# Left-over second products dealt in quarters between the first Strassen products, four eviction buffers in the last groups, and the last WO halves interleaved

## Chip, cores and metric

The kernel runs on one core of one Trainium2 chip. The metric is the device time of one execution in microseconds (us). Three executions of the kernel before took 1122.71, 1125.68 and 1120.59 us, so the median is 1122.71 us. "Profiled time" is the time of the one execution that was recorded, and "span" is the stretch from its first to its last recorded instruction.

## The reference

The kernel computes, for one sequence of 2048 rows of 576 numbers in float32,

```
xn  = layernorm(x)
out = x + attention(xn) @ wo + relu(xn @ w1) @ w2
```

`w1` is 576 x 4608 and `w2` is 4608 x 576. The attention has 32 heads of 18 columns. A row attends to itself and to seven earlier rows at distances 2, 4, ..., 14, so its scores are products and sums on VectorE and not matrix products. `wqkv` is 576 x 1728 and `wo` is 576 x 576.

## The kernel before

**Tiling.** The rows fall into two phases of 1024 rows (`ph` 0 and 1), a phase into four row blocks of 256 (`tb`), and the 4608 hidden columns into 36 chunks of 128 (`f`). Every float32 matrix product is done as three products of a rounded high part and a remainder (`hi*hi`, `hi*lo`, `lo*hi`). `two` (L172 to L176) makes such a pair from a staged tile: ScalarE copies the high part, and VectorE, or GpSimd where it says `pooled`, subtracts it to get the low part.

**First and second products.** The first product gives `h = relu(xn @ w1)` for a chunk; the second product adds `h @ w2` of the chunk into a `po` accumulator in PSUM. A row block's second product is cut into columns 0 to 255 (`h` = 0) and 256 to 575 (`h` = 1, 320 columns). `evict` (L730) copies the two parts of a finished block into an `ev` buffer with ScalarE (L736); after the second part GpSimd issues a transfer that adds the buffer to the output in HBM (L742). There are two `ev` buffers, and two pairs of `po` banks.

**Two stages in a phase.** The first six chunks are done one by one: 24 slots, numbered `b` to `b` + 23, in each of which `o_two` does one second product. The other 30 chunks are done in pairs of chunks and pairs of row blocks by a Strassen scheme: 30 groups in a phase, each with seven products `M(1)` to `M(7)` and remainders `R` for the rows 512 to 575 of `w1`, all accumulated in PSUM banks called a, q (tiles `ph`), f, r (tiles `pm`). `seed` copies one bank into another (ScalarE, L1006), `keep` copies a bank into SBUF (L1010), `plus` adds a bank to that copy (VectorE, L1015), `c_parts` makes the relu pair of a finished quarter (L783 and L787).

**Rows of the array.** TensorE holds two products at once: one in its lower 64 rows, one in the upper 64. They are issued alternately as pairs. When a bank was last written from one half and is to be written from the other, `rows` (L146) and `mm_rows` (L136) put an instruction ahead that waits until the last such product is complete. Where other work lies between the two, nothing is waited for.

**Order.** There is no scheduler: each engine executes in the order in which the program text emits its instructions. `prologue` (L1170) is the change from the first stage to the second, once in each phase; the first products of group 0 are there, with the second products of the last two slots `n0` and `n0` + 1, which are left over. `group` does groups 1 to 29 in eight steps each, where a second product of a former group lies between two steps. `run_bg` (L667) emits attention work for VectorE (L575, L578 and so on) as long as a running estimate says that VectorE is not more than a margin behind TensorE; `room` computes the margin inside a group. `tail_end` and `last_group` finish a phase: `seam` calls them in phase 0, `epilogue` in phase 1. Their pieces of the last two groups fill `ev` buffers, and `last_group` also took a tile of pool `pr`, free by then, as two more. `epilogue` then does the product with `wo` for four blocks of attention rows, each in two column parts and each part in two halves (`wo_half`, L705). The first two blocks go through `wo_block`; the last two end in `last_part`, which adds on VectorE (L1377) to rows read back from the output and writes them.

**The start.** SP issues the loads in program order: `x` tiles (`load_x`, L301), `w1` (L193), `w2` chunks (`w2_load`, L217). The `w2` chunks go through two staging buffers, so the third waits until chunk 0 is split.

## Time and profile before

| what | value |
|---|---|
| median of three executions | 1122.71 us |
| profiled time | 1121.96 us |
| its span | 1119.9 us |
| TensorE busy | 1105.7 us |
| VectorE, ScalarE, GpSimd busy | 844.5, 573.1, 358.8 us |
| granted TensorE clock | 1.00 in every slice |
| HBM traffic | 152 GB/s over the span |

Lines of a view by time begin with the start and the length in us; "idle before" in brackets is how long the engine stood idle and what ended that. PE is TensorE, PEld its weight loads, DVE VectorE, ACT ScalarE, POOL GpSimd; a q behind the name is the engine's sequencer or queue. One row of a matmul is one half of a pair; two halves start together. In a stream without waits pairs of 256 columns start every 0.11 us and pairs of 320 columns every 0.15 us, so a wait shows as a larger distance between two starts even where the engine is called busy, because a recorded matmul lasts 0.27 us.

### The profile page before, as it was taken

Reading aid. Unit: us, or ns where it says so; the run is one execution under the profiler, and the core shown is the slowest. Engines: PE = TensorE matmul, PEld = TensorE weight load, DVE = VectorE, ACT = ScalarE, POOL = GpSimd, SP = SyncE. Lnnn points to the kernel's source line nnn. Section 1 sums busy time; section 2 is a strip of 40 time slices with the busy share of each in tenths; the row PEclk is TensorE's granted clock in tenths of the full one; section 3 lists DMA queues with packets and bytes.
Section 4 is the critical chain, followed back from the end, with each engine's and each line's share of the span. In section 5 each row is a group of like instructions: output and inputs, shape, how many; then the busy total and the mean of one; then the engine's idle time right before and its main releaser. Section 6 shows DMA issues by size and latency. Waiting matters only on the chain.

```text
span 1119.9 us, 37923 instructions
## 1 busy us (share of the span) xinstructions
PE 1105.7 (99%) x16410; PEld 1089.5 (97%) x16410; DVE 844.5 (75%) x1254; ACT 573.1 (51%) x1350; POOL 358.8 (32%) x377
## 2 busy tenths in 40 slices
PE   8999999999999999999999999999999999999998
PEld 8999999999999999999999999999999999999988
DVE  6676798897897898985326339988988988989551
ACT  5434563564465355567544345636635644565550
POOL 2314341333333233443211225314413323334421
PEclk9999999999999999999999999999999999999999
DMA  7369995696597588889957257749857956988895
GB/s 234 129 162 223 188 183 101 143 203 110 118 222 131 88 201 154 148 164 270 267 80 171 38 126 164 143 80 216 166 97 159 194 94 147 181 146 164 180 209 137
DMA packets 136598, 177.26 MB, mean 158 GB/s; under 512 B 27872, under 2 KB 83936, under 8 KB 136400
## 3 DMA queue, kind: packets, MB, share of 16 engines
q0 software_dynamic: 37632, 81.40, 46.8%
q1 hardware_dynamic: 98080, 92.55, 28.1%
q8 instruction: 129, 2.11, 0.7%
q10 hardware_dynamic: 720, 0.89, 0.2%
q14 instruction: 37, 0.30, 0.1%
HBM read 74.07 MB, written 96.22 MB: 152 GB/s over the span
## 4 chain that ended last, share of the span: by engine, by line
PE 87%; DVE 4%; issue 4%; DMA 2%; ACT 2%; POOL 1%; DVEq 0%; ACTq 0%; POOLq 0%
PE po L163 28%; PE po L142 22%; PE ph L163 14%; PE pm L163 11%; PE pm L142 5%; PE ph L142 4%; DMA out<-ev 2%; PE ph L130 1%; DVE ar L176 1%; PE po L130 1%; DVE ar L787 1%; DVE att L622 1%; PE po L119 0%; DMA st<-in_w 0%; ACT ev L736 0%
## 5 line engine op out<-in xcount | busy, mean ns | idle before, releaser
L163 PE MATMUL po<-ar 64*128 64x320 f32 (+1 forms) x5760 | 456.8, 289 | 1.8 <-ACT ar L783 1.7
L163 PEld LDWEIGHTS po<-ar 64*128 64x128 f32 x5760 | 398.7, 184 | 3.3 <-ACT ar L783 1.9
L163 PE MATMUL ph<-xT,ar 64*128 64x256 f32 x2520 | 319.8, 275 | 2.6 <-ACT pm L1006 1.3
L742 POOL DMA_DIRECT2D out<-ev x128 | 151.6, 1184 | 486.6 <-ACT ev L736 376.2
L163 PEld LDWEIGHTS ph<-xT,ar 64*128 64x128 f32 x2520 | 285.7, 184 | 5.7 <-ACT pm L1006 3.5
L163 PE MATMUL pm<-xS,ar 64*128 64x256 f32 x2160 | 258.8, 275 | 0.6
L163 PEld LDWEIGHTS pm<-xS,ar 64*128 64x128 f32 x2160 | 236.1, 184 | 1.9 <-ACT u L1010 0.6
L736 ACT ACTIVATE ev<-po 128x512 f32<-128x512 f32 (+1 forms) x266 | 171.5, 651 | 128.1 <-PE po L163 65.6
L176 DVE TENSOR_TENSOR ar<-st,ar 128x256 fp32r<-128x256 f32 (+3 forms) x236 | 156.4, 675 | 73.7 <-ACT ar L172 73.2
L172 ACT ACTIVATE ar<-st 128x256 fp32r<-128x256 f32 (+3 forms) x304 | 149.1, 504 | 12.1 <-DMA st<-in_w 4.7
L142 PE MATMUL po<-wq,xT 64*128 64x432 f32 x1296 | 133.8, 353 | 0.3 <-ACT ev L736 0.3
L142 PEld LDWEIGHTS po<-wq,xT 64*128 64x128 f32 x1296 | 119.9, 184 | 3.2 <-ACT ev L736 0.6
L938 POOL TENSOR_TENSOR st<-st 128x256 f32<-128x256 f32 x120 | 113.2, 949 | 16.0 <-DVE ar L787 6.5
L174 POOL TENSOR_TENSOR ar<-st,ar 128x256 fp32r<-128x256 f32 (+1 forms) x68 | 75.7, 1116 | 126.3 <-ACT ar L172 126.3
L163 PE MATMUL ph<-xS,ar 64*128 64x256 f32 x720 | 102.7, 275 | 1.3 <-ACT ph L1006 1.1
L163 PEld LDWEIGHTS ph<-xS,ar 64*128 64x128 f32 x720 | 94.2, 184 | 2.8 <-ACT ph L1006 2.1
L610 DVE TENSOR_TENSOR pr<-att 128x1152 f32<-128x1152 f32 x64 | 87.1, 1378 | 0.6
L575 DVE TENSOR_TENSOR pr<-att 128x1152 f32<-128x1152 f32 x64 | 87.2, 1367 | 0.2
L578 DVE TENSOR_REDUCE att<-pr 128x64 f32<-128x1152 f32 x64 | 85.6, 1342 | 0.0
L142 PE MATMUL po<-ar 64*128 64x256 f32 (+1 forms) x984 | 71.1, 289 | 0.0
L617 DVE TENSOR_TENSOR pr<-pr 128x1152 f32<-128x1152 f32 x64 | 70.0, 1094 | 1.2
L787 DVE SCALAR_TENSOR_TENSOR ar<-ph,ar 128x256 fp32r<-128x256 f32 x96 | 39.0, 418 | 40.6 <-ACT ar L783 40.2
(120 smaller groups left out, 1365.7 us busy)
## 6 DMA issues: line engine op xcount, KB each, us to landing
out<-ev POOLq DMA_DIRECT2D x128, 576.0 KB, 7.2
st<-in_w SPq DMA_DIRECT2D x72, 288.0 KB, 5.8
st<-in_w SPq DMA_DIRECT2D x63, 256.0 KB, 3.5
att<-att SPq DMA_DIRECT2D x16, 441.0 KB, 4.4
att<-in_wqkv SPq DMA_DIRECT2D x28, 216.0 KB, 6.8
od<-att SPq DMA_DIRECT2D x32, 160.0 KB, 4.8
att<-in_x SPq DMA_DIRECT2D x14, 288.0 KB, 4.1
st<-in_w SPq DMA_DIRECT2D x60, 64.0 KB, 6.4
```

What stands on the lines that cost most here:

```text
L142: ins = nc.tensor.matmul(o, l[z], r[z], start=start, stop=stop)
L163: b.ins = nc.tensor.matmul(b.ap, l[part], r[part], start=start, stop=stop, skip_group_check=skip)
L172: nc.scalar.activation(hi, src, AF.Copy)
L174: nc.gpsimd.tensor_tensor(lo, src, f32(hi), op=ALU.subtract)
L176: nc.vector.tensor_tensor(lo, src, f32(hi), op=ALU.subtract)
L575: nc.vector.tensor_tensor(pr[i], q, window(k, i), op=ALU.mult)
L578: nc.vector.tensor_reduce(lg[:, i], pr.pop(i).rearrange(heads, d=Dh), axis=AX.X, op=ALU.add)
L610: nc.vector.tensor_tensor(pr[i].rearrange(heads, d=Dh), e, window(v, i).rearrange(heads, d=Dh), op=ALU.mult)
L617: nc.vector.tensor_tensor(o, z[:, :, 0:n], z[:, :, n : 2 * n], op=ALU.add)
L736: nc.scalar.activation(acc[:, :, cols], z[:, :, 0 : cols.stop - cols.start], AF.Copy)
L742: ADDED[ph, tb] = nc.gpsimd.dma_start(rows_of(ph, tb), acc, accum_op=ALU.add)
L938: nc.gpsimd.tensor_tensor(stg(o), stg(a), stg(b), op=op)
```

## The change

- In `prologue`, `o_two(n0)` and `o_two(n0 + 1)` are cut into quarters of three pairs (parts 0 and 2 have 256 columns, parts 1 and 3 have 320) and dealt between the group's products. The margins of `run_bg` there are other ones, and group 1 has one more due time in `room`.
- `w2_split` of chunk 7 comes later in the prologue, behind the last part of slot `n0`, whose `w2` copy it overwrites.
- The `pr` tile is taken at the start of `tail_end` and serves for pieces 2 and 3 of the last two groups (row blocks 0 and 2). The last group's pieces 0 and 1 go to an `ev` buffer.
- In `epilogue`, the last two blocks do both first halves before both second halves.
- At the start, `w2_load(0, 2)` stands ahead of the loads of `x` tiles 4 to 7.

```diff
@@ o_two
-    def o_two(n):
+    def o_two(n, parts=range(4)):
...
-        hi, lo = H.pop(n)
+        hi, lo = H[n]
...
-        if f == 0:
+        if f == 0 and 0 in parts:
             o_tiles(n)
...
-        for j in range(4):
+        for j in parts:
             k, h = divmod(j, 2)
             behind = PB[j - 2] if j > 1 else PB[3] if j == 0 and f else None
             PB[j] = mm_rows((run(k, h, False), run(1 - k, h, True)), behind)
-        o_out(n, by_part=True)
+        if 3 in parts:
+            del H[n]
+            o_out(n, by_part=True)
@@ prologue
-        o_two(n0)
+        o_two(n0, (0,))
...
         rows(M(ph, g, 5, last=True), M(ph, g, 1, last=True))
         seed(ph, g, "q", "a")
         keep(ph, g, "m5", "f")
-        run_bg(1.0)
+        run_bg(-0.8)
...
-        o_two(n0 + 1)
+        o_two(n0, (1, 2))
...
         rows(M(ph, g, 2), M(ph, g, 6))
...
+        o_two(n0, (3,))
         rows(M(ph, g, 6, last=True), M(ph, g, 2, last=True))
         seed(ph, g, "r", "q")
-        run_bg(-0.8)
+        run_bg(0.3)
+        o_two(n0 + 1, (0, 1))
         rows(R(ph, g, 0, 0), R(ph, g, 1, 1))
         c_parts(ph, g, 0, 0, bank(ph, g, "a"))
...
+        o_two(n0 + 1, (2,))
         rows(M(ph, g, 3), M(ph, g, 7))
+        run_bg(0.0)
+        o_two(n0 + 1, (3,))
         rows(M(ph, g, 7, last=True), M(ph, g, 3, last=True))
         keep(ph, g, "u3", "r")
@@ group, room
-            run_bg(room(i, True))
+            run_bg(room(i, True, prev == 0))
...
-    def room(i, half):
+    def room(i, half, first=False):
         now = (i - 1) * STEP + 0.7 if half else i * STEP
-        return min(next(d for d in DUE if d > now + 0.01) - now, 2.5)
+        due = sorted(DUE + (2.0 * STEP,) * first)
+        return min(next(d for d in due if d > now + 0.01) - now, 2.5)
@@ tail_end
         g = NG - 1
+        z = prp.tile([P, 2, 2, D], F32, name="pr")
+        EV[ph, 2 * ((g - 1) % 2), "o"] = z[:, 0], []
+        EV[ph, 2 * (g % 2), "o"] = z[:, 1], []
@@ last_group
-        z = prp.tile([P, 2, 2, D], F32, name="pr")
-        for j in range(2):
-            EV[ph, 2 * (g % 2) + j, "o"] = z[:, 1 - j], []
@@ epilogue
             for h in (1, 0):
                 wo_half(1, 2 + r, h, False)
+            for h in (1, 0):
                 wo_half(1, 2 + r, h, True, z[:, r])
@@ the slots
-        late(b + 22, w2_split, ph, 7, (0, 1), True)
+        on(ph, 0, 5, "O", w2_split, ph, 7, (0, 1), True)
@@ the start
+    w2_load(0, 2)
     for i in range(4, NI):
         load_x(i)
-    w2_load(0, 2)
```

SP's queue at the start, one piece of the difference (`st_163` is `w2` chunk 1, `st_217` and `st_213` are the staging of chunk 2, `att<-in_x` x4 are the `x` tiles 4 to 7):

```order
 L301 DMA att<-in_x 128x576
 L217 DMA st_163<-in_w 128x576
+L217 DMA st_213<-in_w 128x576
 L301 DMA att<-in_x 128x576 x4
-L217 DMA st_217<-in_w 128x576
 L200 DMA st<-in_w 128x4x384
```

The load of chunk 2 moved ahead of four `x` loads, which now wait on SP behind it.

TensorE in the prologue of phase 0, at the end of `M(2)`/`M(6)`, before (`x2` is the last half pair of the one block and the first of the next):

```order
L163 MATMUL ph<-xT,ar 128x256
L163 MATMUL ph<-xS,ar 128x256 x2
L163 MATMUL ph<-xT,ar 128x256
L163 MATMUL ph<-xS,ar 128x256
L163 MATMUL ph<-xT,ar 128x256
```

and after:

```order
L163 MATMUL ph<-xT,ar 128x256
L163 MATMUL ph<-xS,ar 128x256
L142 MATMUL po<-ar 128x320 x6
L163 MATMUL ph<-xS,ar 128x256
L163 MATMUL ph<-xT,ar 128x256
```

Three pairs of a left-over second product now stand where the two blocks met. At the four other places where blocks of the prologue meet stand one or two parts as well; before, the two left-over products stood whole at the first two of the five places.

ScalarE in the same prologue, before (`st_1448` is chunk 7 of `w2`, `st` the staged Strassen matrices, L1006 the seeds, L1010 the copies m5 and u3, L736 the evictions of row block 3):

```order
L172 ACTIVATE ar<-st_1448 128x256
L172 ACTIVATE ar<-st_1448 128x320
L172 ACTIVATE ar<-st 128x2x256
L1006 ACTIVATE ph<-ph 128x256
L1010 ACTIVATE m_2017<-pm 128x256
L736 ACTIVATE ev<-po 128x2x256
L736 ACTIVATE ev<-po 128x2x320
L172 ACTIVATE ar<-st 128x2x256
L1006 ACTIVATE pm<-ph 128x256
L783 ACTIVATE ar<-ph 128x256
L1010 ACTIVATE u_2134<-pm 128x256
```

and after:

```order
L172 ACTIVATE ar<-st 128x2x256
L1008 ACTIVATE ph<-ph 128x256
L1012 ACTIVATE m_1993<-pm 128x256
L172 ACTIVATE ar<-st 128x2x256
L1008 ACTIVATE pm<-ph 128x256
L783 ACTIVATE ar<-ph 128x256
L172 ACTIVATE ar<-st_1448 128x256
L172 ACTIVATE ar<-st_1448 128x320
L736 ACTIVATE ev<-po 128x2x256
L736 ACTIVATE ev<-po 128x2x320
L1012 ACTIVATE u_2134<-pm 128x256
```

The split of chunk 7 and both evictions moved from ahead of the seeds to between the relu of quarter (0, 0) and the copy u3.

TensorE in the last WO block, before (rows of one half stand together: 320 columns first half, 320 second half, 256 first half, 256 second half):

```order
L142 MATMUL po<-wq,xS 128x320 x20
L142 MATMUL po<-att,xS 128x320 x4
L142 MATMUL po<-wq,xS 128x320 x2
L142 MATMUL po<-att,xS 128x320 x2
L142 MATMUL po<-wq,xS 128x320 x20
L142 MATMUL po<-att,xS 128x320 x4
L142 MATMUL po<-wq,xS 128x320 x2
L142 MATMUL po<-wq,xS 128x256 x20
L142 MATMUL po<-att,xS 128x256 x4
L142 MATMUL po<-wq,xS 128x256 x2
L142 MATMUL po<-att,xS 128x256 x2
L142 MATMUL po<-wq,xS 128x256 x20
```

and after:

```order
L142 MATMUL po<-wq,xS 128x320 x20
L142 MATMUL po<-att,xS 128x320 x4
L142 MATMUL po<-wq,xS 128x320 x2
L142 MATMUL po<-att,xS 128x320 x2
L142 MATMUL po<-wq,xS 128x256 x20
L142 MATMUL po<-att,xS 128x256 x4
L142 MATMUL po<-wq,xS 128x256 x2
L142 MATMUL po<-att,xS 128x256 x2
L142 MATMUL po<-wq,xS 128x320 x20
L142 MATMUL po<-att,xS 128x320 x4
L142 MATMUL po<-wq,xS 128x320 x2
L142 MATMUL po<-wq,xS 128x256 x20
```

The first half of the 256 columns moved between the two halves of the 320 columns, and the second half of the 320 columns between those of the 256.

More of the change, by code (lines that the diff above doesn't have):

```diff
@@ L1246, in step @@
                 f(*a)
-            run_bg(room(i, False))
+            run_bg(room(i, False, prev == 0))
         late_after = {
```

## The prediction

> **What bounds the kernel now.** I read the page's head first, then the busy time by stretches, then the chain of waits. In the head the reader is to see that TensorE is the bound from end to end, and in the stretches that its idle time lies in short places.
>
> ```profile
> PE 1105.7 (99%) x16410; PEld 1089.5 (97%) x16410; DVE 844.5 (75%) x1254; ACT 573.1 (51%) x1350; POOL 358.8 (32%) x377
> ```
>
> ```profile
> core 0: us, PE busy (x) PEld busy (x) DVE busy (x) ACT busy (x) POOL busy (x), PEclk, DMA share, GB/s
> ...
> 113.00:121.00 8.00, 7.38 (x101) 6.27 (x99) 6.12 (x16) 3.67 (x10) 2.31 (x3) 1.00 1.08 174
> ...
> 664.00:671.00 7.00, 6.44 (x89) 5.53 (x89) 5.08 (x9) 2.73 (x9) 1.03 (x1) 1.00 0.95 193
> ```
>
> The two stretches are the prologues of the phases. Each holds about 0.6 us of idle TensorE, and both look alike. The change takes no matmul away, so it can only win what TensorE waits. The chain, at its start and near its end, shows two waits on transfers:
>
> ```profile
> 13.73 5.29 DMA st<-in_w
> ...
> 19.51 2.35 PE po L130 x12
> ```
>
> ```profile
> 1067.72 10.40 DMA out<-ev
> ...
> 1079.18 4.44 PE po L163 x58
> ```
>
> The first is the load of `w2` chunk 2: it lands at 19.02 and releases the third second product. In the second, an output transfer holds an `ev` buffer until 1078.12; ScalarE's eviction stands behind it, and the relu that TensorE needs stands behind the eviction.
>
> **Part 1, the early load of chunk 2.** TensorE's rows around it:
>
> ```profile
> 14.52 0.27 PE L355 MATMUL ph<-ident,att 128*64 128x128 f32 x1
> 14.55 3.38 PE L130 MATMUL po<-ar 128*128 128x256 f32 x24
> 17.77 0.60 PE L354 MATMUL pm<-ident,att 128*128 128x128 f32 x4
> 18.20 0.27 PE L355 MATMUL ph<-ident,att 128*64 128x128 f32 x1
> ...
> 21.70 3.34 PE L130 MATMUL ph<-xT,ar 128*128 128x256 f32 x28
> ```
>
> The two second products before it took 17.77 - 14.55 = 3.22, so 1.61 each, and began 0.03 behind a transpose. The third needs 18.20 + 0.03 + 1.61 = 19.84, and its successor began at 21.70: 1.86 us are lost.
>
> ```profile
> SPq L217 <- DVE ar L787: 2.9, 1, 2.9
> ```
>
> SP waits for the staging buffer in both orders, and the load is issued at 13.73 either way. Before, it had four `x` loads ahead of it. After, nothing is ahead. How long will it take? Bounds by the nearest transfers of the same 288 KB, three lone writes from 26 us on and the `w1`/`w2` loads of the first 14 us:
>
> ```profile
> out<-ev SPq DMA_DIRECT2D x3, 288.0 KB, 2.1
> ```
>
> ```profile
> st<-in_w SPq DMA_DIRECT2D x3, 288.0 KB, 4.6
> ```
>
> I take 2.1, since the queue ahead is empty: the load lands at 15.8. The splits end 1.3 us behind the landing at 19.02,
>
> ```profile
> 19.48 0.85 DVE L176 TENSOR_TENSOR ar<-st,ar 128x256 fp32r<-128x256 f32 x2 [2.72 <-ACT ar L172]
> ```
>
> so they end before 18.2 if VectorE comes to them by 17.3, and all 1.86 us go. At 4.6 the load lands at 18.3, 0.7 us earlier than now, and 0.7 go. Nothing in it excludes the middle. The Trainium skill ("DMA: Bandwidth & Descriptors", section "Queues, rings and completion order") says that on each DMA engine the descriptors of one queue are consumed in ring order. By that rule the four `x` loads issued behind chunk 2 cannot hold it and the sum is the full one; by the 4.6 us of the row above it would be 1.2 us less. No row here separates the two.
>
> What is moved back are the `x` loads and, by their 1.85 us of issue, the `w1` and `wqkv` loads behind them:
>
> ```profile
> 9.08 1.85 SPq L301 DMA_DIRECT2D att<-in_x  x4
> ```
>
> The `x` loads go from 9.08 to about 14.1. The first reader of an `x` tile among them is
>
> ```profile
> 22.30 0.82 DVE L313 BATCH_NORM_STATS2 bst<-att 128x6 f32<-128x288 f32 x2
> ```
>
> which comes to 20.4 with the gain. Tile 4 issued at 14.1 has 6.3 us for that; it lands at 17 by the 2.1 and its place behind chunk 2, at 18.7 by the 4.6. I cost it at nothing; should it take 6.9 as in the first 14 us, 0.6 is lost.
>
> **Part 2, the quarters.** At the three places where two blocks of a prologue meet (phase 0, upper or lower rows of `ph` alone):
>
> ```profile
> 113.32 0.27 PE L163 MATMUL ph<-xT,ar 64*128 64x256 f32 x1
> ...
> 113.67 0.38 PE L163 MATMUL ph<-xT,ar 64*128 64x256 f32 x1
> 113.89 0.27 PE L163 MATMUL ph<-xT,ar 64*128 64x256 f32 x1
> ...
> 114.34 0.27 PE L163 MATMUL ph<-xT,ar 64*128 64x256 f32 x1
> ...
> 115.82 0.27 PE L163 MATMUL ph<-xT,ar 64*128 64x256 f32 x1
> ...
> 116.18 0.38 PE L163 MATMUL ph<-xT,ar 64*128 64x256 f32 x1
> ```
>
> Against a pitch of 0.11 the first change of rows costs 0.35 - 0.11 = 0.24 and 0.11 more at the second pair. The block after 114.34 begins at 114.79, so 0.34 and, by the same restart, some 0.1. The third costs 0.25 and 0.11. Together 1.13 us a prologue, 2.26 in both. Is a quarter enough cover? The wait needs 0.35 from the last pair's start. Three pairs of 256 put the next pair 4 x 0.11 = 0.45 behind. The left-over product itself changes rows after three pairs and shows no wait:
>
> ```profile
> 108.96 1.72 PE L142 MATMUL po<-ar 64*128 64x256 f32 x24
> 110.51 0.28 PE L163 MATMUL pm<-xS,ar 64*128 64x256 f32 x1
> ```
>
> Its 12 pairs took 1.55 = 6 x 0.11 + 6 x 0.145, nothing more. So I take the whole 2.26.
>
> What loses its cover: the seeds lay behind a whole product of 1.55. The seed behind the pair at 114.34 shows what they need:
>
> ```profile
> 114.65 0.37 ACT L1006 ACTIVATE pm<-ph 128x256 f32<-128x256 f32 x1 [0.41 <-PE ph L163]
> ```
>
> 0.31 + 0.37 = 0.68 us from the last pair's start, some 0.05 more to release TensorE. Behind the first seed now stand parts 1 and 2, and the next block starts 0.11 + 0.78 = 0.89 behind that pair: 0.15 to spare, and that only because ScalarE no longer has the split of chunk 7 ahead of the seed. Behind the second stand parts 0 and 1, `R` and part 2: ample. That split and the evictions now stand between relu (0, 0) and the copy u3:
>
> ```profile
> 108.04 0.91 ACT L172 ACTIVATE ar<-st 128x256 fp32r<-128x256 f32 x2 [0.44 <-PE po L142]
> ...
> 112.52 1.19 ACT L736 ACTIVATE ev<-po 128x512 f32<-128x512 f32 x2 [0.24 <-PE po L142]
> ...
> 117.19 0.38 ACT L1010 ACTIVATE u<-pm 128x256 f32<-128x256 f32 x1 [1.37 <-PE pm L163]
> ```
>
> Counted on from 108.96 with 0.69 for a block of six pairs, 0.34 and 0.44 for the parts and 0.34 for `R`, `R` ends at 113.70 and the prologue at 115.85. Relu (0, 0), 0.38 long, then ends at about 114.3, the split (0.91) at 115.2, the evictions (1.19) at 116.3, while the copy could start at 116.05. It is late by 0.25; who waits for it is `M(4)` in step 2 of group 1, which comes at 115.85 + 0.69 + 0.24 = 116.8, when a copy of 0.38 is just done. I cost it at nothing; without that slack it is 0.2 a prologue. The waits for rows in steps 2 to 4 of group 1, where nothing lies between, stay. The attention product that `room` moves behind step 2 frees the subtraction ahead of it; neither lies on TensorE's path.
>
> **Part 3, four buffers.** Piece 2 of group 28 goes to the `pr` tile, so ScalarE waits for no transfer. Its next wait is what TensorE delivers.
>
> ```profile
> 1076.36 1.14 PE L163 MATMUL po<-ar 64*128 64x320 f32 x12
> ```
>
> ```profile
> 527.25 1.14 PE L163 MATMUL po<-ar 64*128 64x320 f32 x12
> 528.23 0.28 PE L142 MATMUL pm<-xT,ar 64*128 64x256 f32 x1
> ```
>
> In phase 0 (second fence) the same six pairs were followed by the next work 0.98 later. In phase 1 they start at 1076.36, so TensorE was ready at 1077.34 and began at 1079.18: 1.84. Late subtractions cost about 0.3 in the block behind, as TensorE followed ScalarE closely. Late next is the eviction of piece 3: the piece ends at 1077.5, an eviction of 640 takes
>
> ```profile
> 1079.28 0.71 ACT L736 ACTIVATE ev<-po 128x640 f32<-128x640 f32 x1
> ```
>
> so its banks are free at 1078.25, and the second piece of the last group wants them at 1077.34 + 0.69 = 1078.03: 0.22 and a restart of 0.11. Net 1.84 + 0.3 - 0.33 = 1.8. Piece 1's eviction needs the old `ev` buffer free at 1078.12; it comes at about 1080.2. Phase 0 shows no such stall, so nothing is won there.
>
> **Part 4, WO halves.** Each half of the last two blocks waits for its own first half:
>
> ```profile
> 1102.47 0.30 PE L142 MATMUL po<-att 64*128 64x320 f32 x2
> 1102.84 0.56 PE L142 MATMUL po<-wq,att 64*128 64x320 f32 x4
> ```
>
> ```profile
> PEld po L142 <- PE po L142: 1.2, 4, 0.3
> ```
>
> 0.37 instead of 0.15 and a restart of 0.11, four times: 1.3 us. With another half between, nothing is waited for. The banks: the next block's first half needs those that `last_part` frees, whose two additions take
>
> ```profile
> 1112.85 0.89 DVE L1377 TENSOR_TENSOR xS<-po,xS 128x320 f32<-128x320 f32 x2 [3.53 <-PE po L142]
> ```
>
> 1.2 behind the half, against 1.5 of the half that now follows. The last write still starts behind the last addition, with the other part's write up to 1.4 us ahead instead of 3.4; I allow 0.1 for that, either way.
>
> **Sum.** 1.86 + 2.26 + 1.8 + 1.3 = 7.2 us. Against the profiled 1121.96 (2.1 of it outside the span) that is 1114.8; the median lies 0.75 above, which would give 1115.5. I say 1115.0.
>
> **Rivals.**
> - *Only the matmul order wins.* Chunk 2 still lands late (0.7) and an output transfer still holds ScalarE in the last groups, at the `ev` buffer that piece 1 takes. Then 0.7 + 2.26 + 1.3 = 4.3 and 1117.7. For it speak the 4.6 us row and the 10.40 us of the transfer; against it, that the `ev` buffer has 2 us to spare.
> - *The quarters don't hide the waits*, because ScalarE's seeds bind instead: 2.26 less, 1117.1. Against it stands an idle ScalarE, for it that 0.15 us is thin.
> - *Absorbed in the middle.* TensorE reaches the attention stretches of both phases earlier, and VectorE is the late one there: the 1.86 + 2.26 of the starts go into longer waits, 1118.9 remains. Against it, VectorE has 25% idle and takes most of its start times from TensorE.
> - *Slower.* The output transfers fall into other phases against the evictions.
>
> ```profile
> ACT ev L736 <- DMA out<-ev: 9.4, 13, 2.0
> ```
>
> That is ScalarE's wait for them between 121 and 1070 us, nearly all harmless now. In the tail, 1.84 of 4.24 us reached TensorE. If all of it reached TensorE, 9.4 - 7.2 = 2.2 us are lost, 1124.2; it turns the sign from three quarters on. Against it: groups 2 to 28 keep their order, and the transfers are issued by the same evictions.
>
> **How the numbers follow.** About 0.5% (5.6 us) is what a measurement of this kernel can tell from no change. Forecast 0.64; only the matmul order 0.12; quarters without effect 0.07; absorbed 0.12; slower 0.05. Of the forecast's cases nearly all pass 1117.1, since the bounds of part 1 take 1.2 and those of the copy 0.4; the second and third lie at that border or short of it, the fourth short of it. So faster 0.66, same 0.30, slower 0.04. The forecast's own range is 1113 to 1117; the shown runs spread by 2.5 around their median. The range goes from 1111.8 (0.4 of scatter in the middle's waits and a fast run) to 1119.2, which takes in the first three rivals.
>
> **What would show it.** In the profile after: the first matmul of the third second product near 18.3 with no idle time before it, and the load of chunk 2 landing near 16; busy TensorE with no idle of its own between the blocks of both prologues; no wait of ScalarE's eviction on an output transfer in the last 55 us, and about 0.3 us in front of the last group's second piece; no wait of TensorE on itself in the last 20 us. The prediction is wrong if statistics of tile 4 wait for its load, if a seed or u3 shows as a releaser of TensorE in the prologues, or if waits between 121 and 1070 us grow by more than 2 us.

## The result, and the profile after

The changed kernel takes 1115.52 us (median of nine runs, 1113.76 to 1118.52), the kernel before 1120.59 us in the runs beside it. The ratio is 0.9949, with a 95% interval of 0.9933 to 0.9965: faster by about 5 us. The profiled execution took 1115.52 us, its span 1113.7 us against 1119.9. So the two profiled executions lie 6.4 us apart and the medians 5.1, since the profiled execution of before was 1.4 us slower than the median that more runs gave it (1120.6). About 1 us of the 6.4 has nothing to do with the change: by the distance between the same two instructions, the profiled execution of before spent 0.9 to 1.3 us more between 300 and 450 us than each of the other thirteen executions profiled here, a second one of the same kernel among them.

The head of the page after. In both heads PE is busy 99% of the span; PE busy falls by 4.0 us and the span by 6.2.

```profile
PE 1101.7 (99%) x16410; PEld 1090.9 (98%) x16410; DVE 846.6 (76%) x1254; ACT 572.1 (51%) x1350; POOL 358.4 (32%) x377
```

**The start.** TensorE's rows around the third second product, and ScalarE's split of `w2` chunk 2:

```profile
18.14 0.27 PE L355 MATMUL ph<-ident,att 128*64 128x128 f32 x1
18.17 1.86 PE L130 MATMUL po<-ar 128*128 128x256 f32 x12
```

```profile
17.22 0.78 ACT L172 ACTIVATE ar<-st 128x256 fp32r<-128x256 f32 x2 [1.81 <-DMA st<-in_w]
```

The product follows the transpose by 0.03 us without idle time. The split waited for the landing until 17.2, not 15.8. Two traces are compared below by the distance between the same two instructions; over the start the distance shrank by 1.72 us.

**The prologues.** The seam of two blocks of phase 0, with a quarter between them:

```profile
112.86 0.27 PE L163 MATMUL ph<-xT,ar 64*128 64x256 f32 x1
112.86 0.27 PE L163 MATMUL pm<-xS,ar 64*128 64x256 f32 x1
112.97 0.59 PE L142 MATMUL po<-ar 64*128 64x320 f32 x6
113.41 0.28 PE L163 MATMUL pm<-xS,ar 64*128 64x256 f32 x1
```

Pairs follow each other at 0.11 (256 columns) and 0.15 (320 columns), also across the change of rows: 113.41 - 112.97 = 0.44 = 3 x 0.147. Phase 0's prologue is 1.17 us shorter and phase 1's 1.21. The copy u3 is named as the releaser of TensorE's weight load in step 2 of group 1, with 0.32 us after and with 0.32 us before, so it costs nothing more. But in phase 1 a new wait follows at once, in step 5 of group 1. GpSimd's and VectorE's rows there, then ScalarE's:

```profile
663.18 3.63 POOL L940 TENSOR_TENSOR st<-st 128x256 f32<-128x256 f32 x4
```

```profile
663.25 1.28 DVE L787 SCALAR_TENSOR_TENSOR ar<-u,ar 128x256 fp32r<-128x256 f32 x1 [0.48 <-ACT ar L783]
```

```profile
664.95 0.37 ACT L1008 ACTIVATE ph<-ph 128x256 f32<-128x256 f32 x1 [1.73 <-DVE m L1017]
```

A subtraction that takes 0.42 us elsewhere took 1.28 beside a GpSimd addition that had started 0.07 us earlier. VectorE's next addition came late, the seed behind it also, and TensorE lost 0.56 us (0.45 and a restart of 0.11). Below this is called the collision.

**Near the end of phase 1.** The waits between 1055 and 1065 us (columns: engine, line, what it waited for; us in total, times, longest), and TensorE's row that carries the last one:

```profile
ACT wq L172 <- DMA att<-wo: 3.0, 1, 3.0
PEld ph L163 <- ACT ph L1008: 1.6, 1, 1.6
PE ph L163 <- ACT ph L1008: 1.4, 1, 1.4
```

```profile
1062.69 0.38 PE L163 MATMUL ph<-xS,ar 64*128 64x256 f32 x1 [1.35 <-ACT ph L1008]
```

This is another new wait. ScalarE stands at the split of the first `wo` tile until the tile has landed, and the seed of the last group's second step is queued behind it. TensorE lost 1.5 us here where it had lost 0.24 before.

**The last groups.** The row of the 4.24 us wait in the kernel before, then ScalarE's rows that answer to it:

```profile
1078.22 0.60 ACT L736 ACTIVATE ev<-po 128x512 f32<-128x512 f32 x1 [4.24 <-DMA out<-ev]
```

```profile
1071.59 0.60 ACT L736 ACTIVATE pr<-po 128x512 f32<-128x512 f32 x1 [0.80 <-PE po L163]
1072.31 0.42 ACT L783 ACTIVATE ar<-m 128x256 fp32r<-128x256 f32 x1
1074.24 0.39 ACT L783 ACTIVATE ar<-pm 128x256 fp32r<-128x256 f32 x1 [1.51 <-PE po L163]
1074.52 0.70 ACT L736 ACTIVATE pr<-po 128x640 f32<-128x640 f32 x1
```

In this execution the evictions go to `pr` and wait for TensorE only. From the last regular group to the product with `wo` the time is 1.6 us shorter. The eviction of piece 3 (last row) stands behind a relu and comes 0.28 us later than the prediction had it, so the last group's second piece waits 0.46 + 0.11 us and not 0.33. In the product with `wo`, the waits from 1095 us on hold no PE or PEld any more:

```profile
DVE xS L1386 <- PE po L142: 22.7, 4, 16.6
POOL out L745 <- ACT ev L736: 5.3, 1, 5.3
ACT ev L736 <- PE po L142: 1.3, 1, 1.3
```

### The profile page after: what moved, and what is told of

Read it like the earlier page. It is cut to its first block, busy times and chain, and to the rows that moved or that the text cites. A ratio compares the mean times of both kernels' runs of the same rounds, so it can differ in the third digit from the quotient of the medians.

```text
span 1113.7 us, 37923 instructions
## 1 busy us (share of the span) xinstructions
PE 1101.7 (99%) x16410; PEld 1090.9 (98%) x16410; DVE 846.6 (76%) x1254; ACT 572.1 (51%) x1350; POOL 358.4 (32%) x377
## 4 chain that ended last, share of the span: by engine, by line
PE 90%; DVE 4%; issue 2%; ACT 2%; DMA 1%; SPq 0%; POOL 0%; DVEq 0%; ACTq 0%; POOLq 0%
PE po L163 29%; PE po L142 22%; PE ph L163 15%; PE pm L163 11%; PE pm L142 5%; PE ph L142 4%; PE ph L130 1%; DVE ar L176 1%; PE po L130 1%; DVE ar L787 1%; DVE att L622 1%; DMA od<-att 1%; PE po L119 0%; ACT ev L736 0%; DVE pr L610 0%
## 5 line engine op out<-in xcount | busy, mean ns | idle before, releaser
L163 PE MATMUL po<-ar 64*128 64x320 f32 (+1 forms) x5760 | 486.6, 289 | 0.4 <-ACT pr L736 0.3
L163 PEld LDWEIGHTS po<-ar 64*128 64x128 f32 x5760 | 428.8, 184 | 1.6 <-PE po L163 0.5
L163 PEld LDWEIGHTS ph<-xT,ar 64*128 64x128 f32 x2520 | 289.4, 184 | 4.7 <-ACT pm L1008 3.0
L163 PE MATMUL pm<-xS,ar 64*128 64x256 f32 x2160 | 262.1, 275 | 0.5
L163 PEld LDWEIGHTS pm<-xS,ar 64*128 64x128 f32 x2160 | 239.7, 184 | 1.3 <-ACT u L1012 0.6
L736 ACT ACTIVATE ev<-po 128x512 f32<-128x512 f32 (+1 forms) x266 | 171.8, 651 | 127.1 <-PE po L163 71.7
L142 PE MATMUL po<-wq,xT 64*128 64x432 f32 x1296 | 137.6, 353 | 0.0
L142 PEld LDWEIGHTS po<-wq,xT 64*128 64x128 f32 x1296 | 125.3, 184 | 1.0
L617 DVE TENSOR_TENSOR pr<-pr 128x1152 f32<-128x1152 f32 x64 | 70.1, 1095 | 1.2
```

Of the source, the lines that this page charges most:

```text
L142: ins = nc.tensor.matmul(o, l[z], r[z], start=start, stop=stop)
L163: b.ins = nc.tensor.matmul(b.ap, l[part], r[part], start=start, stop=stop, skip_group_check=skip)
L617: nc.vector.tensor_tensor(o, z[:, :, 0:n], z[:, :, n : 2 * n], op=ALU.add)
L736: nc.scalar.activation(acc[:, :, cols], z[:, :, 0 : cols.stop - cols.start], AF.Copy)
```

## The experiments

The profiled executions differ by more than one of the parts is worth, so each run is read twice: by its times, and by the distances between the same instructions in its trace.

### Each part undone

**The early load undone.**

```diff
-    w2_load(0, 2)
     for i in range(4, NI):
         load_x(i)
+    w2_load(0, 2)
```

> The changed kernel, with the load of w2 chunk 2 again behind the loads of x tiles 4 to 7. Two theories. (A) The start is a plain gain: the idle time of TensorE ahead of the third second product comes back (1.7 us, from the two traces: 42.37 against 40.65 us at the end of the first blocks) and is handed on to the end. Then the span is 1.7 us longer than that of the changed kernel (1113.7), 1115.4, and it is 0.4% faster than before. (B) The start is absorbed: the attention stretches take the same absolute time whether TensorE comes 1.7 us earlier or later. Then the 1.7 us is seen at 42 us and gone by 215 us, and the span is 1113.7 to 1114.2.

Measured: 1116.38 us (eight runs, 1113.44 to 1118.19), span 1113.7. Neither theory: TensorE lost 0.69 us at the start and not 1.7. The transfer of chunk 2 was shorter than in the trace of before. Its row in the view of transfers (KB, us from issue to landing), in the kernel before, in the changed kernel and in this run:

```profile
st<-in_w SPq DMA_DIRECT2D x1, 288.0 KB, 5.3
```

```profile
st<-in_w SPq DMA_DIRECT2D x1, 288.0 KB, 3.6
```

```profile
st<-in_w SPq DMA_DIRECT2D x1, 288.0 KB, 4.2
```

So the 1.86 us of the prediction came from one execution. The 0.69 reached the attention stretch of phase 0 undiminished; that the span is not longer comes from later places (no collision at 665 us, 0.94 in place of 1.5 us at 1062).

**The old prologue.**

```diff
-        o_two(n0, (0,))
+        o_two(n0)
...
-        o_two(n0, (1, 2))
+        o_two(n0 + 1)
...
-        o_two(n0, (3,))
...
-        o_two(n0 + 1, (0, 1))
```

and so on, with the old margins of `run_bg` and `room` and the old place of the split of chunk 7.

> The changed kernel, with the prologue of before: whole left-over products, old margins of the attention work, split of chunk 7 in its old place. (A) The quarters hide the waits for rows and nothing else: each prologue is 1.15 to 1.2 us longer. The new wait of 0.56 us in group 1 of phase 1 is made by the earlier start of GpSimd's first Strassen matrix, which falls on a subtraction of VectorE: the old order has that start 8 us later, so the wait is gone. Together 1.15 + 1.2 - 0.56 = 1.8 us more by 700 us, a span of 1115.5. (B) The wait of 0.56 us is not of the order's making (it belongs to the place in group 1): it stays, and 2.3 us more stand, a span of 1116.0. (C) The wait of 1.5 us of phase 1 near 1062 us is made by the other margins too: then it is gone as well and the span is 1114.3.

Measured: 1117.81 us (ten runs), span 1115.5. The prologues are 1.20 and 1.19 us longer, each against an execution without the collision. GpSimd's first Strassen addition of phase 1 started at 669.23, the subtraction took 0.42, and the wait in group 1 was gone, as in (A). The wait near 1062 us was gone too, as in (C). But 0.87 us were lost 9 us later, where ScalarE waited for attention rows and the copy u3 stood behind that:

```profile
ACT att L697 <- DMA att<-od: 1.4, 1, 1.4
ACT pr L736 <- PE po L163: 0.7, 1, 0.7
PEld pm L163 <- ACT u L1012: 0.7, 1, 0.7
```

That the span is the 1115.5 of (A) is chance: the wait near 1062 us, absent here, is worth 1.4 us the other way, and the losses that (A) did not have, this one and 0.6 us in the stretches between, make up for it.

**The old buffers.**

```diff
     def tail_end(ph, more):
-        z = prp.tile([P, 2, 2, D], F32, name="pr")
-        EV[ph, 2 * ((g - 1) % 2), "o"] = z[:, 0], []
-        EV[ph, 2 * (g % 2), "o"] = z[:, 1], []
...
     def last_group(ph, more=lambda k: None):
+        z = prp.tile([P, 2, 2, D], F32, name="pr")
+        for j in range(2):
+            EV[ph, 2 * (g % 2) + j, "o"] = z[:, 1 - j], []
```

> The changed kernel, with the eviction buffers of before in the last groups. (A) The wait on the output transfer comes back in phase 1: the stretch from the last regular group (1073 us) to the product with wo is 1.6 us longer, ScalarE's eviction of a piece waits for an output transfer again, and the span is 1115.3. Phase 0 does not change. (B) The 1.84 us wait of before was an accident of when that one transfer was served: then no such wait, and the span stays at 1113.7, even 0.5 us less, since the wait that came in its place (0.56 us) goes too.

Measured: 1116.64 us (nine runs), span 1114.5. ScalarE did wait for the output transfer again, but only so long:

```profile
1074.01 0.60 ACT L736 ACTIVATE ev<-po 128x512 f32<-128x512 f32 x1 [2.53 <-DMA out<-ev]
```

It cost TensorE nothing: from the last regular group to the product with `wo` the time was that of the changed kernel within a few hundredths of a us, since the relu behind this eviction has to wait for TensorE's piece in any case. The times say 1.1 us more, with a standard error of 0.5. In the profiled execution neither theory holds whole: the wait is there, as in (A), and costs nothing, as in (B). Its span is 0.8 us longer for losses elsewhere, 0.3 of them at the start. Why the times still differ, the later runs suggest.

**The old order of the halves.**

```diff
             for h in (1, 0):
                 wo_half(1, 2 + r, h, False)
-            for h in (1, 0):
                 wo_half(1, 2 + r, h, True, z[:, r])
```

> The changed kernel, with the halves of the last two blocks of the product with wo as before. (A) Four waits of TensorE's weight loads on TensorE itself come back, 0.3 us each by the trace of before: 1.3 us more between 1079 us and the end, a span of 1115.0. (B) The end is set by the last additions and the last write, not by TensorE: then the waits come back but the span does not move by more than 0.4 us.

Measured: 1117.68 us (nine runs), span 1115.9. The four waits came back, in this run's waits from 1095 us on,

```profile
PEld po L142 <- PE po L142: 1.2, 4, 0.3
```

and the excess of TensorE's distances over their pitch rose by 1.34 us after 1086 us, as in the trace of before. So (A) holds for this part. The span is 2.2 us longer, as 0.7 us were lost at the start too, where chunk 2 took 4.1 us.

The means of the four undo runs lie 0.57, 2.25, 1.07 and 1.73 us above that of the changed kernel (1115.65, 14 runs), with standard errors of 0.5 to 0.6. The sum is 5.6 us; the mean of before in these runs is 5.6 us above as well. So the parts add up as far as this can tell: the mean of the changed kernel enters the sum four times, and its standard error is about 1.7 us.

### How much of it was the draw

**The kernel before, profiled again**, without an edit.

> The kernel before, profiled a second time. The first undo runs lost less than the traces of before and after differ by: the load of chunk 2 behind the four x loads landed at 17.85 there and not at 19.0, and with the old buffers the wait on the output transfer cost nothing. (A) The two waits of before are properties of its order: again more than 1.5 us are lost ahead of the third second product and more than 1.5 us ahead of the last group's second piece. (B) They were the draw of that one execution: the first is 0.6 to 1.2 us with a landing of chunk 2 before 18.4, the second under 0.5 us, and the span is 1.5 to 2.5 us shorter than 1119.9. (C) One of each: the start is a draw, the wait near the end belongs to the order, since the loads of wo and the reads of the attention rows are issued 4 us later in it; the span is 0.7 to 1.2 us shorter.

Measured: 1119.77 us, span 1117.7, so 2.2 us shorter. Chunk 2 took 4.5 us and the third second product lost 1.45 us. ScalarE's eviction in the last groups waited 2.52 us, not 4.24, and TensorE lost nothing there:

```profile
st<-in_w SPq DMA_DIRECT2D x1, 288.0 KB, 4.5
```

```profile
1076.03 0.60 ACT L736 ACTIVATE ev<-po 128x512 f32<-128x512 f32 x1 [2.52 <-DMA out<-ev]
```

Closest to (B): the span is in its range, and the stall near the end was a draw, that is, what one execution happened to show. At the start the loss and the landing (18.5) lie between the two theories. Not all of the 2.2 us is in these two places: 1.0 was won between 300 and 450 us, and 0.7 us were lost at 1073 us, where ScalarE waited 1.4 us for attention rows, as in the run with the old prologue. This loss also brings the eviction later and so shortens its wait. (C) falls, since the loads of `wo` were issued late in this execution too (1057.7).

**A lone load of chunk 2, and a swap on ScalarE.**

```diff
-        nc.sync.dma_start(X[0, i], x_v[0, i])
+        ins = nc.sync.dma_start(X[0, i], x_v[0, i])
+        if i == 4:
+            tc.add_manual_dep(ins.ins, W2I[0].ins.name, SYNC, reason="lone")
...
         o_half(ph, g - 1, 3, True)
+        o_evict(ph, g - 1, 3)
         c_parts(ph, g, 1, 0, bank(ph, g, "r"))
         more(2)
-        o_evict(ph, g - 1, 3)
```

> The changed kernel with two edits far apart. First, the load of x tile 4 waits until chunk 2 of w2 has landed, so that nothing is issued behind chunk 2 while it is under way. (A) What is issued behind it does not hold it: it takes 3.5 to 4.1 us as in the four runs with the early load, and the x tiles come 3.5 us later, with statistics of tile 4 waiting near 20.5 us for about 1 us. (B) The followers share the engines with it: it takes 2.1 to 2.8 us. Second, in the end of phase 1 the eviction of piece 3 stands ahead of the relu of bank r. (A) The wait of TensorE ahead of the last group's second piece (0.46 + 0.11 us) falls by 0.28 us, the time that ScalarE spends on that relu first. (B) The relu is late in its place and the wait moves to the piece that reads it: nothing is won.

Measured: 1115.23 us, span 1113.5. Chunk 2 took 4.3 us with nothing behind it. In the executions with the early load and four `x` loads behind it, it took 2.9 to 4.1 (eight of them up to the run below on more cover). So (A), as far as one execution tells: the followers do not hold it. The other half of (A) failed: the statistics of tile 4 came at 21.15 without a wait for the load. The rule that the prediction takes from the Trainium skill ("DMA: Bandwidth & Descriptors", section "Queues, rings and completion order"), that each DMA engine consumes the descriptors of a queue in ring order, is not contradicted; but ring order did not give the 2.1 us. The stretches of this execution (columns: us of the stretch; busy time of the engines; clock; mean share of the 16 DMA engines; GB/s) and the row of one queue between 14 and 15 us (packets, MB, share of 16 engines) show how it ended:

```profile
14.50:15.50 1.00, 1.00 (x10) 1.00 (x9) 0.93 (x5) 0.80 (x3) 0.37 (x1) 1.00 0.89 191
15.50:16.50 1.00, 1.00 (x10) 1.00 (x9) 1.00 (x3) 0.00 (x0) 0.31 (x1) 1.00 0.28 104
16.50:17.50 1.00, 1.00 (x10) 1.00 (x9) 0.13 (x1) 0.00 (x0) 0.00 (x0) 1.00 0.06 16
```

```profile
q8 instruction: 1, 0.02, 10.1%
```

Of the 144 packets of the load 133 had passed by 16.0; the other 11 came one at a time, the last before 17.5, at the share of one DMA engine of 16 (0.06). Meanwhile one packet of instructions, 16 KB, had started between 14 and 15 us and taken 10.1% of 16 us, 1.6 us of one engine. The other early loads fit: with that packet between 14 and 16 us at 1.0 us they took 3.5 and 3.6, at 1.3 to 1.4 us 4.0 to 4.1, and in the two executions in which it came after 16 us, 2.9 and 3.2. So the load seems to end with the engine that also fetches instructions. The rows go together in all of them; no edit moved the fetch, so it isn't shown beyond that. The second edit won 0.19 us, less than the 0.28 of (A): the relu is now 0.6 us later, but nothing moved behind it.

### The two new waits

**GpSimd's additions later, and the last quarter deeper.**

```diff
-                on(ph, a - 2, 8, "O", sw_mix, 0)
...
+                    on(ph, 1, 2, "O", sw_mix, 0, lambda: LOWS[-1])
...
-        o_two(n0 + 1, (2,))
         rows(M(ph, g, 3), M(ph, g, 7))
         run_bg(0.0)
-        o_two(n0 + 1, (3,))
+        o_two(n0 + 1, (2,))
         rows(M(ph, g, 7, last=True), M(ph, g, 3, last=True))
...
+        ins[ph, 1, 1].append((o_two, (b + NOLD - 1, (3,))))
```

> The changed kernel with two edits. First, the four additions of GpSimd for the first pair of Strassen matrices come two steps later and behind VectorE's latest low part, so that they do not start beside the subtraction ahead of M(6). (A) The wait of 0.56 us in group 1 of phase 1 is made by that start (VectorE's subtraction took 1.28 us where it takes 0.42): no such wait in either phase, the subtraction takes 0.42. It was absent in two of the four undo runs too, where GpSimd started a fraction later. (B) The additions then hold VectorE at another place and 0.3 to 0.9 us turn up within the next 10 us. Second, the last quarter of the left-over product goes between steps 1 and 2 of group 1 and the one before it ahead of M7's second half. (A) It covers the wait for rows there, 0.31 + 0.08 us a phase. (B) Its bank is evicted later, and a second product of group 2 or 3 waits for it: nothing is won.

Measured: 1115.30 us, span 1113.3. In phase 1 the moved quarter of this kernel reads `h` after the relu of the copy u3 has overwritten it: the home of the slot's `h`, its place in SBUF, is the one that this relu writes. So in those columns another product is computed, and the quarter waited 0.85 us for that relu:

```profile
PEld po L142 <- ACT ar L785: 0.9, 1, 0.9
PE po L142 <- ACT ar L785: 0.7, 1, 0.7
```

In phase 0 the homes differ, and 0.44 + 0.07 us were won, as in (A). The first edit: GpSimd started at 666.20, the subtraction (now L789) took 0.42, the seed caused no wait, and nothing turned up behind it. (A).

That GpSimd's start is the cause is seen across the runs. In all eight executions with the new prologue and the additions in their old place, the order of the two starts decides. In four, GpSimd had started 0.07 to 0.21 us ahead, and the subtraction took 1.27 or 1.28 us; in four, VectorE was ahead by 0.05 to 0.46, and it took 0.42 or 0.43. One of each, from the run with the old buffers and from that with the late load (GpSimd's row, VectorE's row):

```profile
663.82 3.76 POOL L940 TENSOR_TENSOR st<-st 128x256 f32<-128x256 f32 x4
```

```profile
664.03 1.27 DVE L787 SCALAR_TENSOR_TENSOR ar<-u,ar 128x256 fp32r<-128x256 f32 x1 [0.48 <-ACT ar L783]
```

```profile
664.35 4.47 POOL L940 TENSOR_TENSOR st<-st 128x256 f32<-128x256 f32 x4
```

```profile
664.30 0.42 DVE L787 SCALAR_TENSOR_TENSOR ar<-u,ar 128x256 fp32r<-128x256 f32 x1 [0.48 <-ACT ar L783]
```

The Trainium skill ("SBUF — State Buffer", section "Who interferes with whom") says that a VectorE instruction with two inputs in SBUF contends with a GpSimd instruction that reads SBUF, and that the order of issue decides which of the two blocks. The traces agree: `u` and `ar` both lie in SBUF, and in all four executions with the long subtraction it ended 0.29 us after the one GpSimd addition that had started ahead of it.

**The splits of `wo` later.**

```diff
-            z.append((("ws", kt), wo_split, (ph, kt), None, (("wl", 13 + 3.0 * (kt - 2)),)))
+            z.append((("ws", kt), wo_split, (ph, kt), None, (("wl", 13 + 3.0 * (kt - 2) + 3.0 * ph),)))
```

> The changed kernel, with the splitting of wo in phase 1 put 3 us later in the row of the attention's tasks (of ScalarE and VectorE). (A) The wait of TensorE near 1062.7 us (1.5 us in the changed kernel, 0.9 to 1.7 in the runs since) comes from ScalarE, which stands at the split of the first wo tile until that tile has landed, with a seed queued behind it: then the wait falls to the 0.24 us of the kernel before, the split waits less than 0.5 us, and 0.7 to 1.3 us are won by the end of the last regular group. (B) The stretch is bound by transfers or VectorE anyway: the wait moves to a later product (as in the run with the old prologue, where 0.63 us stood 9 us later) and at most 0.4 us is won.

Measured: 1119.20 us, span 1117.4. The wait near 1062 us was gone, and that point came 1.6 us earlier relative to 1042. Then, as in (B), 1.06 us were lost at 1069 us. ScalarE waited for an output transfer, and the copy u3 behind it for ScalarE:

```profile
ACT ev L736 <- DMA out<-ev: 1.1, 1, 1.1
PEld pm L163 <- ACT u L1012: 1.0, 1, 1.0
```

And a loss that neither theory had: the attention's tasks are emitted one at a time, so the split of the last attention block fell behind the last evictions and additions on ScalarE and VectorE, and TensorE lost 4.4 us near the end (the longest of its waits from 1095 us on):

```profile
PEld po L142 <- ACT xS L697: 2.7, 2, 2.3
```

### Half of the change, and a better version

**The changed kernel again**, in the rounds of the two runs that follow.

> The changed kernel again, in the same rounds as the two that follow, to compare them directly. If the draw of the transfers sets its scatter, its median lies between 1115 and 1116.5 and single times spread by 4 to 5 us; the third second product starts 2.9 to 3.0 us at the least after the second and otherwise by the landing of chunk 2, between 3.2 and 4.3 us after its issue.

Measured: 1115.94 us (five runs, 1113.99 to 1117.47), span 1114.2. Chunk 2 took 4.0 us, and 0.48 us were lost at the start. The collision and the wait near 1062 us were absent. The times spread by 3.5 us, less than the 4 to 5 expected. And 0.6 us were lost near 1070, where ScalarE waited for an output transfer one eviction before the first that the `pr` tile serves:

```profile
1068.19 0.60 ACT L736 ACTIVATE ev<-po 128x512 f32<-128x512 f32 x1 [1.11 <-DMA out<-ev]
```

So the prediction's sign "no wait of ScalarE's eviction on an output transfer in the last 55 us" is met in one of the two profiled executions of the changed kernel and not in the other.

**Only the quarters and the halves of `wo`**: the edits of the late load and of the old buffers above, together.

> Only the quarters and the interleaved halves of wo: the load of chunk 2 and the eviction buffers are those of before. (A) By the parts as predicted, the early load and the four buffers are worth 1.86 + 1.8 = 3.7 us: 3.7 us above the changed kernel in the same rounds. (B) By the traces since, the early load is worth about 1 us (chunk 2 landed 4.2 to 5.3 us after its issue behind the x loads and 3.2 to 4.3 ahead of them) and the buffers between nothing and 1.8, as the transfers fall; with the quarters the loads of wo are issued 4 us earlier and the output transfer came in time with the old buffers. Then 0.8 to 1.8 us above the changed kernel, 1116.5 to 1117.3, 3.3 to 4.1 us below the kernel before.

Measured: 1117.87 us (five runs), span 1116.3; 1.7 us above the changed kernel by the means, 1.9 by the medians of these rounds. (A)'s 3.7 falls. (B)'s amount holds. But its reason for the buffers does not, since the long wait was there:

```profile
1076.01 0.60 ACT L736 ACTIVATE ev<-po 128x512 f32<-128x512 f32 x1 [4.23 <-DMA out<-ev]
```

It cost 1.6 us. So with the old buffers the wait took 4.24, 2.52, 2.53 and 4.23 us in four executions, two with each prologue, and cost 1.6, 0, 0 and 1.6; the transfers waited for took 10.4, 9.5, 8.7 and 10.3 us. With the new buffers no eviction waited for a transfer at that place in any of the ten executions. What stays is the eviction before it, which waited 1.1 us for an output transfer in two of them and cost 0.6 and 1.06 us.

**More cover.** The deeper quarter, the later GpSimd additions and the swap above, together, and

```diff
-BASE = (0, 1000)
+BASE = (0, 1002)
```

which gives the slots of phase 1 other homes of `h`, so that the deeper quarter reads the right one.

> The changed kernel with the edits that won something: the last quarter of the left-over product between steps 1 and 2 of group 1 (0.5 us in phase 0 in the run before; in phase 1 its h is now kept in a home of its own by another count of the slots, so that it doesn't wait for the relu that overwrote it), GpSimd's first Strassen additions behind VectorE's low part, and the eviction of piece 3 ahead of a relu (0.19 us). (A) The three act on their own: 0.5 in each phase, 0.56 of the collision in about half of the executions, 0.2 at the end, 1.2 to 1.7 us below the changed kernel in the same rounds. (B) What is won before 1042 us is taken back by the loads of wo (TensorE's product near 1062 us started 2.91 us behind the landing of the first wo tile in seven of the nine executions looked at): then 0.2 to 0.6 us below. (C) The other count of slots makes a new wait at the seam of the phases, and nothing is won.

Measured: 1115.43 us (six runs, 1113.59 to 1116.89), span 1113.4; 0.6 us below the changed kernel by the means, with a standard error of 0.6. The prologues won 0.44 and 0.96 us and the swap 0.19. By the amount (B) holds, and by its place only in part. At 690 us the kernel was 1.1 us ahead of the changed kernel, at 1042 us 0.3. What had been won went at 953 us, where an output transfer held ScalarE's eviction and TensorE's weight load waited for that (ScalarE's row, then the wait):

```profile
952.65 0.60 ACT L736 ACTIVATE ev<-po 128x512 f32<-128x512 f32 x1 [2.52 <-DMA out<-ev]
```

```profile
PEld po L163 <- ACT ev L736: 0.7, 1, 0.7
```

It cost 0.86 us; in three other executions with the new prologue the same place cost 0.2 to 0.5, in the rest nothing. The wait for the `wo` tile then took 1.3 us, as much as in the changed kernel:

```profile
1059.59 0.69 ACT L172 ACTIVATE wq<-att 128x576 fp32r<-128x576 f32 x1 [2.95 <-DMA att<-wo]
```

TensorE's product started 2.88 us behind the start of that split, at 1062.47. In seven of the nine executions with the new prologue and the split in its place, the one above among them, it followed the split by just this time and had waited, between 0.26 and 1.65 us.

**The split behind the seed.** The same kernel, with one more edit:

```diff
+        if ph:
+            on(ph, NG - 1, 2, "T", wo_split, ph, 2)
...
-        for kt in range(2, KT + 1):
+        for kt in range(2 + ph, KT + 1):
             z.append((("ws", kt), wo_split, ...
```

> The kernel of the last run, with one instruction pair moved: the split of the first wo tile in phase 1 stands behind the seed of the last group's step 2 on ScalarE and VectorE, all else in its place. (A) TensorE's product near 1062 us was bound by the landing of that tile (2.91 us behind it): it now starts without a wait of more than 0.3 us, and up to 1.3 us are won at that point. If nothing takes them back, the kernel is 0.8 to 1.3 us below the last one, 1114.1 to 1114.6. (B) What is won there is taken by the next transfer in the stretch: ScalarE's eviction then waits for an output transfer, and a product near 1069 to 1073 us waits 0.4 to 1.1 us for ScalarE's copy behind it, as in the run in which all splits came later (1.06 us lost there). Then it ends within 0.5 us of the last one.

Measured: 1113.39 us (six runs, 1113.17 to 1114.26), span 1111.2; the ratio to the kernel before is 0.9940, with an interval of 0.9928 to 0.9952. That is 2.1 us below the changed kernel by the means, with a standard error of 0.4. These runs are of other rounds, though, in which the kernel before was 0.9 us faster too; against the kernel before in the same rounds the two gain 6.8 and 5.6 us, so 1.2 apart. In the trace the point came 1.6 us earlier relative to 1042, and nothing took it back. ScalarE's seed waits for TensorE only, and an eviction for an output transfer, but too short to matter:

```profile
1058.23 0.37 ACT L1012 ACTIVATE ph<-ph 128x256 f32<-128x256 f32 x1 [0.18 <-PE ph L163]
1065.36 0.60 ACT L736 ACTIVATE ev<-po 128x512 f32<-128x512 f32 x1 [0.59 <-DMA out<-ev]
```

(A) holds. That the profiled spans lie even 2.2 us apart is in part the loss at 953 us, which this execution did not have. The six times spread by 1.1 us, where those of the last run had spread by 3.3. So the scatter may have come from this wait or from the one at 953 us; no run here tells them apart.

## Why the prediction was right, and where not

The predicted 1115.0 us lies 0.5 below the measured 1115.5, and the direction was right. That it lies so near is luck in part: the forecast saving of 7.2 us was 2.1 too large. Two terms of the sum were mis-sized, and the trace that the sum was taken from happened to be slow in the same two places and, by about 1 us, between 300 and 450 us.

| term | predicted | measured |
|---|---|---|
| early load of chunk 2 | 1.86 | about 0.9 by traces; 0.6 ± 0.6 by undoing it |
| quarters, both prologues | 2.26 | 2.4 in the prologues, less 0.56 in about half of the executions |
| four buffers | 1.8 | 1.6 in two of four executions, 0 in two |
| halves of `wo` | 1.3 | 1.34 |

- **Part 1 failed in its choice between the bounds.** The step "I take 2.1, since the queue ahead is empty" took the lone writes for its price. The load took 2.9 to 4.1 us with the queue ahead empty, so the row of 4.6 us was the nearer one; an instruction fetch on the same DMA engines goes with the length. The loss itself was also read from one execution, with a transfer of 5.3 us. Behind the `x` loads it took 4.2 to 5.3 us in four executions, and 0.7 to 1.8 us were lost, 1.2 in the mean; ahead of them the losses against the trace after were nothing to 0.7 us, 0.3 in the mean. The later `x` tiles cost nothing, as costed: the statistics of tile 4 came at 20.49 without a wait.
- **Part 2 was right to a tenth** (its terms add to 1.15 a prologue, not to the 1.13 that it gives), and no seed shows as a releaser of TensorE inside the prologues. What it lacked is an engine off the path: with the other margins the preparation of the Strassen matrices, and with it GpSimd's first addition, came 8 us earlier, 3 of them against TensorE, and fell on VectorE's subtraction ahead of a seed. "Neither lies on TensorE's path" was said of the moved subtraction and attention product; the moved addition of GpSimd was not counted at all.
- **Part 3 had the mechanism and its price**, the 1.84 us. It mis-sized how often it is paid: the term was priced from the one execution at hand, and two in four do not pay it. It also took ScalarE to be free of transfers from there on, and one eviction earlier it is not always. The late piece 3 was 0.28 us later than worked out, since the relu that stands ahead of its eviction has itself to wait.
- **Part 4 was right**, its banks and its end too.
- **The rivals.** "Only the matmul order wins" came nearest in the run that had just that: 1.7 us above the changed kernel by the means and 2.3 by the medians of all runs, 2.9 forecast. "Absorbed in the middle" was true of another place than it named: in the profiled execution the gains arrive undiminished at 1042 us, in four others 0.2 to 0.9 us went at 953 us behind an output transfer, and from 1042 to 1063 up to 1.3 us go into the wait for `wo`.

By these sizes the sum is 0.9 + 2.4 - 0.3 + 0.8 + 1.34 = 5.1 us, against the median of 1120.6 that gives 1115.5. The prediction took 7.2 from an execution 1.4 us above that median. The two errors went against each other. The new sum closes better than it should: it leaves out the wait near 1062 us and, on the other side, the 0.7 to 0.9 us that two of the three executions with the old prologue lost near 1073.

## What to carry to other kernels

A wait on a transfer that a profile shows once is a draw: profile the kernel twice before pricing it, and take the mean over what the wait can be, not the one seen. An instruction that waits for a load should not stand in an engine's queue ahead of one that the bound engine needs; moving that one pair behind the seed won 1.6 us in the trace, as much as the four buffers in the executions in which they won anything. When work is moved, look at every engine whose start it moves, also one that is never on the critical path.

## What the runs showed of the hardware

- Which of GpSimd and VectorE starts first, by as little as 0.05 us, decides whether a subtraction of 128x256 with two operands in SBUF takes 0.42 or 1.27 us (four executions of each kind).
- A load of 288 KB with nothing ahead of it and nothing behind it took 4.3 us, its last packets at the share of one DMA engine. One packet of 16 KB of instructions took 1.6 us of an engine meanwhile, and 0.9 to 1.4 us in the other executions.
- Transfers issued between 1040 and 1090 us took 2.1 to 14.1 us from issue to landing in these executions, so what a wait on one of them costs changes from one execution to the next.
